# Layer two's K projection at one Strassen level for seven pairs of token tiles instead of four, and the layer norm of its last tiles applied by ScalarE

## The chip, the cores and the metric

The kernel runs on one core of a Trainium2 chip. The core has five engines, and each works through a queue of its own in program order: TensorE (PE, with its weight loads shown apart as PEld), VectorE (DVE), ScalarE (ACT), GpSimd (POOL) and SyncE (SP), which here issues all transfers to the 16 DMA engines. Work is passed between the engines by semaphores. PSUM is the memory into which TensorE writes, eight banks of 128x512 values in f32; SBUF is the working memory ("arena" in the profile).

The metric is the device time of one launch in microseconds (us), lower being better. The time before is 1434.43 us, the median of three runs.

## The reference, cut to what matters

Two blocks, linear attention (A) and a gated bilinear unit (B), each behind a layer norm and with a residual, are run twice with the same weights. There are 2048 tokens of 1024 features.

```python
def _A_ref(x, wqkv, wo):                      # x is normalised
    q, k, v = split(x @ wqkv)                 # 32 heads of 32
    phi = lambda t: jnp.where(t > 0, t + 1, jnp.exp(t)) + 1e-6
    pq, pk = phi(q), phi(k)
    kv = jnp.einsum("bhsd,bhse->bhde", pk, v)
    z = jnp.einsum("bhsd->bhd", pk)
    num = jnp.einsum("bhqd,bhde->bhqe", pq, kv)
    den = jnp.einsum("bhqd,bhd->bhq", pq, z)[..., None] + 1e-6
    return merge_heads(num / den) @ wo

def _layernorm(x, axis=-1, eps=1e-5):
    m = jnp.mean(x, axis=axis, keepdims=True)
    v = jnp.var(x, axis=axis, keepdims=True)
    return (x - m) / jnp.sqrt(v + eps)

x = A_x
x = x + _A_ref(_layernorm(x), A_wqkv, A_wo)
x = x + _B_ref(_layernorm(x), B_w_gate, B_w_up, B_w_down)
x = x + _A_ref(_layernorm(x), A_wqkv, A_wo)
x = x + _B_ref(_layernorm(x), B_w_gate, B_w_up, B_w_down)
```

## The kernel before

**How the program is put together.** Python code calls `P.add(engine, ...)` for every piece of work, with the memory that it reads and writes. The order of these calls is the order of each engine's queue; the waits between engines follow from the memory ranges. Nothing reorders a queue later. So where an instruction stands in the code decides what stands behind it.

**The stage that the change touches** is the projection of K and Q in layer two, `kq_pairs(0)` (L1025) under `layer_A` (L963). The 2048 tokens are 16 tiles of 128, taken in the order 4, 5, 6, 7, 0 to 3, 12 to 15, 8 to 11, two at a time: pairs 0 to 7. A pair is done in one of two ways.

- `plain` (L1101): four steps, one for each tile and each half of 512 output columns. A step is eight matmuls of 128x512 (`proj2`, L969), an exponential on ScalarE (`ex`, L1062) and, for the K side, one pair of VectorE instructions of 128x1024 for each tile (`fin2_`, L1077: the minimum, L657, and the sum that gives phi, L1085).
- `strassen` (L1151): one Strassen level, seven steps of four matmuls (L1167), in the order of products 1, 5, 6, 2, 7, 3, 4. Banks A, B, C and D of PSUM hold the four blocks. Step 0 multiplies into A, and ScalarE copies A to B (L1179 for K, L1177 for Q). Step 1 multiplies into C with a difference of weight blocks, T(0), and ScalarE copies C to SBUF (`p5`, L1183). Step 2 adds to B, and VectorE's `join` (L1171) writes D = B + `p5`. Step 3 adds to A, which is then complete. Step 4 adds to B and `join` writes C = B + `p5`. Step 5 adds to D, step 6 to B. Each complete block gets an exponential on ScalarE and, one block at a time, the minimum (L657 for K, L655 for Q's first block; Q's other three need none) and phi (L1096) on VectorE (`fin1_`, L1090).

TensorE may go on from step 2 to step 4 only when the first `join` has read B, and from step 4 to step 6 only when the second `join` has. A `fin` isn't put on VectorE's queue at once: it waits in a list (`pend`), and is queued after the next K or Q step, or ahead of any step numbered 0 (`flush`).

Before the change, K pairs 0 to 3 are plain (`KP0 = 4`), K pairs 4 to 7 and Q pairs 0 to 6 go by Strassen. The order is written out in `KQ_SEQ[False]` (L199). A token is one call: `K21` is step 1 of K pair 2, `Q` likewise; `S20` to `S23` are VectorE's four sums of token blocks for pairs 2 and 3 (`s_sums`, L1127); `X` loads a normalised tile back from DRAM; `V`, `W` and `O` load the next weights; `L` is one step of layer norm.

**A step of layer norm** (`flow_step`, L641, of class `LN`) works on four tiles at once, each a stage apart: it starts the transfer that transposes one tile, applies the norm to the next (`ln_b2`, L505), works out the variance of the one after that (`ln_b1`, L490) and the sum of a fourth (`ln_a`, L468). In this stage the sum (L473) and the sum of squares (L493) are ScalarE's, the few 128x1 values between them GpSimd's (L475, L495, L497), and the application is VectorE's (L507). Elsewhere a tile whose statistics come from VectorE is applied by ScalarE (L511). `lnp.on_act` chooses between the two, read when `ln_b1` is queued. When the stage begins, tile 8 (counted in the order above) is being applied, tile 9 has its variance and tile 10 its sum; tiles 10 to 15 are finished by the first eight `L` of the stage, and the others find nothing to do.

**The weight differences T(0) to T(3)** were worked out once in layer one and stored to DRAM (`pt_scratch`). Layer two loads them at the end of the block before it (`dticks1`, `load_t`), Q's four and then K's four, K's in two transfers of 1024 KB: T(0) with T(1), T(2) with T(3). SyncE issues them behind 3.5 MB of other weights and Q's four differences, and ahead of eight stores of x.

**The other place** is the output stage of layer one (L1488 to L1507), where `nxt.on_act` is true and the last tiles' sums already come from ScalarE (`nxt.stat_act = first and i > 11`). There too `ln_b2` took VectorE's L507 whenever the statistics were ScalarE's.

Of the kernel before, what the change touches and what calls it, by code (L numbers as in the profile page):

```python
# [180 lines left out]
def build_kernel(nc, A_x, A_wqkv, A_wo, B_w_gate, B_w_up, B_w_down, out):  # L181
# [14 lines left out]
    KSTR = True  # L196
    NEB = 3
    KQ_SEQ = {True: "L S30 Q20 S31 T L K30 S32 K31 L K32 Q21 S33 L Q22 K33 T S40 Q23 Q30 K40 K41 S41 L K42 Q31 Q32 Q33 L S42 K43 L Q34 K50 L Q35 Q36 S50 S43 K51 L Q40 L S51 S52 K52 Q41 Q42 Q43 L K53 Q44 Q45 L K60 Q46 K61 S60 Q50 S53 K62 Q51 S61 Q52 S62 Q53 Q54 K63 Q55 Q56 K70 Q60 K71 Q61 S63 Q62 L K72 Q63 Q64 Q65 K73 Q66 V",
              False: "K00 S00 S01 K01 S02 S03 L K02 K03 K10 L X K11 Q00 K12 Q01 X L Q02 K13 Q03 Q04 K20 X S20 Q05 S21 K21 S22 L Q06 S23 Q10 K22 X Q11 Q12 K23 Q13 L K30 X Q14 S40 Q15 S41 K31 S42 Q16 S43 Q20 X L K32 Q21 Q22 K33 Q23 X K40 Q24 L K41 Q25 K42 Q26 X K43 Q30 K44 K45 L Q31 K46 X Q32 Q33 K50 Q34 S60 K51 Q35 S61 L X S62 K52 S63 Q36 K53 Q40 K54 Q41 X K55 Q42 L K56 Q43 K60 Q44 K61 X Q45 K62 Q46 K63 L Q50 K64 X Q51 K65 Q52 K66 Q53 K70 L X Q54 K71 Q55 K72 Q56 K73 X Q60 K74 L Q61 K75 Q62 K76 Q63 X Q64 L Q65 Q66 V W O"}  # L199
    L1P0 = 3  # L200
    L1QS = 3
    QLAG = 0.409
# [3 lines left out]
    SPOS = 0.867  # L206
    SSTEP = 0.063
    CUP = 9
    KP0 = 4

    L2SETS = {(False, 0): "15", (False, 1): "15", (True, 0): "1532", (True, 1): "1532"}
    ORDERS = {
# [10 lines left out]
    def take(n, align=64):  # L223
        nonlocal off
        off = (off + align - 1) // align * align
        o = off
        off += n
        return o
# [10 lines left out]
    O_MV = [take(64) for _ in range(8)]  # L239
# [51 lines left out]
    P = _Prog(V_PT + 64)  # L291
# [42 lines left out]
    with ExitStack() as es:  # L334
# [10 lines left out]
        def vb(o, n):  # L345
            return ab[:, o // 2: o // 2 + n]
# [4 lines left out]
        def vf(o, n):  # L351
            return af[:, o // 4: o // 4 + n]
# [31 lines left out]
        mv = [vf(o, 5) for o in O_MV]  # L384
# [37 lines left out]
        def R(o, n):  # L422
            return [(o, o + n)]

        def r_x(i, lo=0, hi=D):
            return [(O_X + (i * D + lo) * 2, O_X + (i * D + hi) * 2)]
# [16 lines left out]
        def mset(ap, v, rng):  # L443
# [5 lines left out]
              rd=R(O_A[0], 1024), pwr=[B_KVT[1]])  # L449
# [8 lines left out]
        for h in range(4):  # L458
# [4 lines left out]
              rd=R(O_IDENT, 256), wr=R(O_IDENT, 256))  # L463
# [26 lines left out]
        def ln_b1(i, j, on_act, act=False, oj=0):  # L490
            junk = vb(oj, D)
            if act:
                P.add("act", lambda e: e.activation(junk, x_res[:, i, :], AF.Square, bias=mv[j][:, 0:1], accum_out=mv[j][:, 1:2]),  # L493
                      rd=r_x(i) + R(O_MV[j], 4), wr=R(oj, D * 2) + R(O_MV[j] + 4, 4))
                P.add("pool", lambda e: e.tensor_scalar(out=mv[j][:, 2:3], in0=mv[j][:, 1:2], scalar1=1.0 / D, scalar2=EPS_LN, op0=ALU.mult, op1=ALU.add),  # L495
                      rd=R(O_MV[j] + 4, 4), wr=R(O_MV[j] + 8, 4))
                P.add("pool", lambda e: e.tensor_tensor(out=mv[j][:, 3:4], in0=mv[j][:, 2:3], in1=mhalf, op=ALU.pow),  # L497
                      rd=R(O_MV[j] + 8, 4) + R(O_MHALF, 4), wr=R(O_MV[j] + 12, 4))
                return
            if on_act:  # L500
                P.add("dve", lambda e: e.tensor_scalar(out=mv[j][:, 4:5], in0=mv[j][:, 0:1], scalar1=mv[j][:, 3:4], scalar2=-1.0,
                                                        op0=ALU.mult, op1=ALU.mult),
                      rd=R(O_MV[j], 4) + R(O_MV[j] + 12, 4), wr=R(O_MV[j] + 16, 4))

        def ln_b2(i, j, dst, r_dst, on_act, act=False):  # L505
            if act:
                P.add("dve", lambda e: e.tensor_scalar(out=dst, in0=x_res[:, i, :], scalar1=mv[j][:, 0:1], scalar2=mv[j][:, 3:4],  # L507
                                                        op0=ALU.add, op1=ALU.mult),
                      rd=r_x(i) + R(O_MV[j], 4) + R(O_MV[j] + 12, 4), wr=r_dst)
            elif on_act:  # L510
                P.add("act", lambda e: e.activation(dst, x_res[:, i, :], AF.Identity, bias=mv[j][:, 4:5], scale=mv[j][:, 3:4]),  # L511
                      rd=r_x(i) + R(O_MV[j] + 12, 8), wr=r_dst)
            else:
                P.add("dve", lambda e: e.tensor_scalar(out=dst, in0=x_res[:, i, :], scalar1=mv[j][:, 0:1], scalar2=mv[j][:, 3:4],
                                                        op0=ALU.subtract, op1=ALU.mult),
                      rd=r_x(i) + R(O_MV[j], 4) + R(O_MV[j] + 12, 4), wr=r_dst)
# [446 lines left out]
        def layer_A(lnp, nxt, first, pro):  # L963
# [61 lines left out]
            def kq_pairs(p0):  # L1025
# [234 lines left out]
                else:  # L1260
                    for p in range(NP_):
                        st_ = plain("k", p) if p < KP0 else strassen("k", p)
                        for n, f in enumerate(st_):
# [4 lines left out]
                    for p in range(0, NP_, 2):  # L1268
                        for n in range(4):
                            at((p - SPOS if p >= KP0 else p + 1 - SPOS) + SSTEP * n, "S%d%d" % (p, n), lambda p=p, n=n: s_do(p, n, 2))  # L1270
                    for n in range(14):
# [56 lines left out]
                lnp.start(2)  # L1328
            else:
                lnp.use_dma = True  # L1330
            lnp.stat_act = not first

            def pt_ops(n):
                w = "kq".index(n)
# [1010 lines left out]
```

## Time and profile before

| what | value |
|---|---|
| time, median of three runs | 1434.43 us (1433.94 to 1434.46) |
| the profiled execution's own time | 1432.3 us |
| its span, first to last instruction | 1430.6 us |
| PE busy | 1420.2 us, 99% |
| DVE busy | 1167.1 us, 82% |
| ACT busy | 733.5 us, 51% |
| POOL busy | 314.6 us, 22% |
| the K and Q stage of layer two | from 730.24 us to 824.23 us of the span |

Starts in a timeline are microseconds from the first instruction. A line of a timeline gives the start, the duration, the engine, the line of the code, the operation, the memory written and read, the number of merged instructions, and, in brackets, how long the engine had been idle before and what ended that. Instructions of one engine overlap a little at their ends, so the cost of one in a full queue is the distance from its start to the next one's start. "idle" of an engine that has nothing to do is no loss; only what holds up the last engine costs time.

### The profile page before, as it was taken

To read this page: it belongs to the slowest core of one execution; us is meant where nothing else is said; L and a number is where in the kernel's file an instruction comes from. 1 tells how busy PE (TensorE), PEld (TensorE's weight loads), DVE (VectorE), ACT (ScalarE), POOL (GpSimd) and SP (SyncE) were. 2 spreads that over 40 slices of the span, in tenths; PEclk is the share of its full clock that TensorE was granted. 3 is DMA by queue.
4 is the path that set the end of the run, shared out by engine and by line. 5 is a ranking of instruction groups with operands and counts; after the bars stand their busy time and mean duration, and the time that the engine had idled before them with its cause. 6 is when DMAs were issued, how large, how long until landed. Compare 5 with 4: busy or idle time off the path is not lost.

```text
span 1430.6 us, 22386 instructions
## 1 busy us (share of the span) xinstructions
PE 1420.2 (99%) x8332; PEld 809.8 (57%) x8388; DVE 1167.1 (82%) x2012; ACT 733.5 (51%) x1538; POOL 314.6 (22%) x321
## 2 busy tenths in 40 slices
PE   9999999999999999999999999999999999999999
PEld 4444444555544555554764444456666477666658
DVE  7878887888879799878778878779877877777886
ACT  4752367767621255552256523667776116777521
POOL 5644632000013000003334346301000400000160
PEclk9999999999999999999999999999999999999999
DMA  6316867987878899985998067589976699788668
GB/s 235 106 28 182 182 137 195 289 294 251 290 253 286 296 324 303 293 260 171 262 355 220 27 178 162 137 229 273 287 253 200 224 299 317 255 261 265 207 187 259
DMA packets 393997, 330.15 MB, mean 231 GB/s; under 512 B 178337, under 2 KB 342049, under 8 KB 393377
## 3 DMA queue, kind: packets, MB, share of 16 engines
q1 hardware_dynamic: 393888, 328.72, 77.0%
q8 instruction: 66, 1.08, 0.3%
q14 instruction: 43, 0.34, 0.1%
HBM read 238.49 MB, written 66.58 MB: 213 GB/s over the span
## 4 chain that ended last, share of the span: by engine, by line
PE 95%; DVE 2%; ACT 1%; issue 1%; POOL 1%; DMA 0%; SPq 0%; ACTq 0%
PE ps L1593 27%; PE ps L1668 18%; PE ps L2109 14%; PE ps L2017 8%; PE ps L1499 8%; PE ps L1401 8%; PE ps L1167 6%; PE ps L971 4%; PE ps L981 2%; PE ps L1413 1%; ACT arena L493 0%; DVE arena L841 0%; DMA arena<-in_A_x_dram 0%; PE ps L1441 0%; ACT arena L473 0%
## 5 line engine op out<-in xcount | busy, mean ns | idle before, releaser
L841 DVE TENSOR_TENSOR arena<-arena 128x512 f16<-128x512 f16 (+9 forms) x780 | 480.5, 644 | 76.4 <-ACT arena L1712 45.1
L1593 PE MATMUL ps<-arena 128*128 128x512 f16 x1808 | 446.8, 379 | 0.6 <-ACT ps L1623 0.6
L1668 PE MATMUL ps<-arena 128*128 128x256 f16 x2324 | 312.1, 273 | 0.7 <-ACT arena L1712 0.6
L844 DVE SCALAR_TENSOR_TENSOR arena<-ps,arena 128x512 f16<-128x512 f32 (+2 forms) x392 | 259.9, 685 | 38.8 <-PE ps L1593 16.3
L1668 PEld LDWEIGHTS ps<-arena 128*128 128x128 f16 (+1 forms) x2324 | 226.4, 98 | 104.0 <-DVE ps L1687 3.8
L1593 PEld LDWEIGHTS ps<-arena 128*128 128x128 f16 (+1 forms) x1808 | 176.5, 98 | 141.7 <-ACT ps L1623 1.1
L2062 POOL TENSOR_TENSOR arena<-arena 128x512 f32<-128x512 f32 x56 | 87.4, 1565 | 596.5 <-ACT arena L2060 591.5
L2109 PE MATMUL ps<-arena 128*128 128x512 f16 (+1 forms) x941 | 205.7, 379 | 0.6
L1598 ACT ACTIVATE arena<-ps 128x512 f16<-128x512 f32 x224 | 134.0, 598 | 91.8 <-PE ps L1593 89.8
L2109 PEld LDWEIGHTS ps<-arena 128*128 128x128 f16 x952 | 93.2, 98 | 111.5
L1684 ACT COPY ps<-ps 128x256 f32<-128x256 f32 x220 | 81.0, 368 | 79.8 <-PE ps L1668 73.4
L1687 DVE TENSOR_TENSOR ps<-ps,arena 128x256 f32<-128x256 f32 x220 | 92.3, 428 | 34.5 <-PE ps L1668 18.3
L2017 PE MATMUL ps<-arena 128*128 128x256 f16 (+1 forms) x1078 | 119.0, 273 | 0.1
L1401 PE MATMUL ps<-arena 128*128 128x512 bf16 x499 | 114.1, 379 | 0.7
L2017 PEld LDWEIGHTS ps<-arena 128*128 128x128 f16 x1078 | 104.9, 98 | 13.9 <-DVE ps L2024 0.4
L1499 PE MATMUL ps<-arena 128*128 128x512 bf16 x500 | 110.7, 379 | 0.6
L2060 ACT ACTIVATE arena<-ps 128x512 f32<-128x512 f32 x48 | 28.7, 597 | 132.6 <-PE ps L2109 132.6
L1167 PE MATMUL ps<-arena 128*128 128x512 bf16 (+1 forms) x412 | 94.7, 379 | 0.8 <-DVE ps L1171 0.3
L1307 POOL TENSOR_TENSOR arena<-arena 128x1024 f16<-128x1024 f32 x32 | 80.0, 2501 | 69.5 <-DVE arena L1305 62.3
L1623 ACT COPY ps<-ps 128x512 f32<-128x512 f32 x112 | 64.2, 573 | 50.2 <-PE ps L1668 44.8
L1006 POOL TENSOR_TENSOR arena<-arena 128x512 f32<-128x512 f32 x60 | 73.6, 1245 | 69.4 <-DVE arena L1096 33.6
L1499 PEld LDWEIGHTS ps<-arena 128*128 128x128 f16 x512 | 50.1, 98 | 59.8
(80 smaller groups left out, 1262.0 us busy)
## 6 DMA issues: line engine op xcount, KB each, us to landing
arena<-w_scratch SPq DMA_DIRECT2D x84, 512.0 KB, 5.2
arena<-sp_scratch SPq DMA_DIRECT2D x56, 512.0 KB, 5.8
arena<-t_scratch SPq DMA_DIRECT2D x27, 896.0 KB, 5.8
arena<-in_B_w_down_dram SPq DMA_DIRECT2D x18, 896.0 KB, 6.2
w_scratch<-arena SPq DMA_DIRECT2D x28, 512.0 KB, 6.0
sp_scratch<-arena SPq DMA_DIRECT2D x28, 512.0 KB, 4.4
arena<-in_B_w_gate_dram SPq DMA_DIRECT2D x42, 256.0 KB, 5.1
arena<-in_B_w_up_dram SPq DMA_DIRECT2D x42, 256.0 KB, 3.4
```

The source lines that it names most:

```text
L841: P.add("dve", lambda e: e.tensor_tensor(out=out, in0=a, in1=b, op=op), rd=rd, wr=wr, prd=prd)
L844: P.add("dve", lambda e: e.scalar_tensor_tensor(out=out, in0=a, scalar=sc, in1=b, op0=ALU.mult, op1=op1), rd=rd, wr=wr, prd=prd)
L1167: P.add("pe", lambda e: [e.matmul(psb(bank), x[:, k, :], w[:, k, :], start=(start and k == 0), stop=(k == 3), skip_group_check=True) for k ...
L1401: return [e.matmul(psb(bank), xr[:, t, j * 128:(j + 1) * 128], pk[:, h, t, :], start=(t == 0), stop=(t == NST - 1)) for t in range(NST)]
L1499: return [e.matmul(psb(bank), xnT[:, g, i * 128:(i + 1) * 128], wp[:, g, dh * 512:(dh + 1) * 512], start=(dh == 0 and g == 0), stop=(g == ...
L1593: P.add("pe", lambda e: [e.matmul(psb(bank), w[:, k, :], x[:, k, :], start=(start and k == 0), stop=(k == 3), skip_group_check=True) for k ...
L1598: P.add("act", lambda e: e.activation(t, psb(bank), AF.Copy, scale=SG), prd=[bank], wr=r)
L1668: P.add("pe", lambda e: [e.matmul(psb(bank)[:, 256 * half:256 * half + 256], w[:, k, :], xx[:, k, :], start=(start and k == 0), stop=(k == ...
L1687: P.add("dve", lambda e: e.tensor_tensor(out=psb(dst[c])[:, 256:512], in0=lo, in1=c5, op=ALU.add), prd=[bk], rd=rc5, pwr=[dst[c]])
L2017: P.add("pe", lambda e: [e.matmul(psb(bank)[:, 256 * half:256 * half + 256], a[:, k, :], w[:, k, :], start=(start and k == 0), stop=(k == ...
L2062: P.add("pool", (lambda k2, x: lambda e: e.tensor_tensor(out=rtmp[k2], in0=rtmp[k], in1=x, op=ALU.add))(k2, x), rd=rx + rr(k), wr=rr(k2))
L2109: return [e.matmul(psb(bank), hv[:, 7 * hf + k, t * 128:(t + 1) * 128], w[:, k, :], start=(start and hf == 0 and k == 0), stop=(hf == 1 an ...
```

## The change

`KP0` becomes 1, so K pairs 1, 2 and 3 go by Strassen too. The written order changes with it. `lnp.on_act` becomes true for the layer norm of layer two's attention, and `ln_b2` obeys it also for tiles whose statistics ScalarE made; `ln_b1` then adds a GpSimd product of two 128x1 values, the bias for ScalarE's instruction.

```diff
     KQ_SEQ = {True: ...
-              False: "K00 S00 S01 K01 S02 S03 L K02 K03 K10 L X K11 Q00 K12 Q01 X L Q02 K13 Q03 Q04 K20 X S20 Q05 S21 K21 S22 L Q06 S23 Q10 K22 X Q11 Q12 K23 Q13 L K30 X Q14 S40 Q15 S41 K31 S42 Q16 S43 Q20 X L K32 Q21 Q22 K33 Q23 X K40 Q24 L K41 Q25 K42 Q26 X K43 Q30 K44 K45 L Q31 K46 X Q32 Q33 K50 Q34 S60 K51 Q35 S61 L X S62 K52 S63 Q36 K53 Q40 K54 Q41 X K55 Q42 L K56 Q43 K60 Q44 K61 X Q45 K62 Q46 K63 L Q50 K64 X Q51 K65 Q52 K66 Q53 K70 L X Q54 K71 Q55 K72 Q56 K73 X Q60 K74 L Q61 K75 Q62 K76 Q63 X Q64 L Q65 Q66 V W O"}
+              False: "K00 S00 S01 K01 S02 S03 L K02 K03 K10 L X K11 K12 X L K13 Q00 K14 S20 K15 S21 Q01 S22 K16 X S23 Q02 Q03 K20 L Q04 K21 Q05 X K22 Q06 K23 X Q10 K24 L K25 S40 Q11 S41 K26 S42 Q12 S43 Q13 K30 X Q14 K31 L Q15 K32 Q16 K33 X Q20 K34 L K35 Q21 K36 X Q22 Q23 K40 Q24 L K41 Q25 X K42 Q26 K43 L Q30 K44 K45 Q31 S60 K46 S61 Q32 X S62 Q33 S63 K50 Q34 L K51 Q35 X K52 Q36 K53 Q40 L K54 X K55 Q41 K56 Q42 Q43 K60 Q44 L K61 Q45 X K62 Q46 K63 L Q50 K64 X K65 Q51 K66 Q52 Q53 K70 L Q54 K71 Q55 K72 X Q56 K73 Q60 X K74 K75 Q61 K76 Q62 Q63 Q64 Q65 Q66 V W O"}
...
-    KP0 = 4
+    KP0 = 1
...
         def ln_b1(i, j, on_act, act=False, oj=0):
...
+                if on_act:
+                    P.add("pool", lambda e: e.tensor_tensor(out=mv[j][:, 4:5], in0=mv[j][:, 0:1], in1=mv[j][:, 3:4], op=ALU.mult),
+                          rd=R(O_MV[j], 4) + R(O_MV[j] + 12, 4), wr=R(O_MV[j] + 16, 4))
                 return
...
         def ln_b2(i, j, dst, r_dst, on_act, act=False):
-            if act:
+            if act and not on_act:
                 P.add("dve", lambda e: e.tensor_scalar(out=dst, in0=x_res[:, i, :], scalar1=mv[j][:, 0:1], scalar2=mv[j][:, 3:4],
                                                         op0=ALU.add, op1=ALU.mult),
...
             elif on_act:
                 P.add("act", lambda e: e.activation(dst, x_res[:, i, :], AF.Identity, bias=mv[j][:, 4:5], scale=mv[j][:, 3:4]),
...
-            lnp.stat_act = not first
+            lnp.stat_act = lnp.on_act = not first
```

## The prediction

> **What bounds the kernel now.** I read the page first, then the chain of waits around layer two's K and Q stage, then the timelines of ScalarE, GpSimd and VectorE in it, then the landing times of the transfers.
>
> ```profile
> PE 1420.2 (99%) x8332; PEld 809.8 (57%) x8388; DVE 1167.1 (82%) x2012; ACT 733.5 (51%) x1538; POOL 314.6 (22%) x321
> ...
> 730.24 10.31 PE ps L971 x47
> ...
> 741.41 1.73 PE ps L971 x8
> ...
> 820.89 3.50 PE ps L1167 x15
> 824.39 6.91 PE ps L1401 x32
> ```
>
> TensorE sets the time, and in this stage it never pauses: the chain stays on it from the first K matmul at 730.24 to the G matmuls that follow. Eight matmuls of 128x512 take 1.73 us, 0.216 each. Everything else in the stage is hidden, so the question is what the change uncovers.
>
> **What it removes.** A plain pair has 32 matmuls, a Strassen pair 28. K pairs 1 to 3 save 12 x 0.216 = **2.6 us**. This is all there is to win, since no other engine ends the stage; and 0.2% of the time, about what a measurement of this kernel can tell from no change, is 2.9 us.
>
> **The weight differences.** Step 1 of a K Strassen pair multiplies with T(0). Before the change the first such step is K41, 208 matmuls into the stage (about 775). Now it is K11, behind K00 to K03 and K10: 36 matmuls, 730.24 + 36 x 0.216 = 738.0. Two rows on each transfer give its issue and the time from there to its landing:
>
> ```profile
> L441 SPq DMA_DIRECT2D arena<-pt_scratch x1: 432/432/432, 731.1 to 731.1; - x1
> DMA to landing us min/median/max: 12.0/12.0/12.0
> ...
> L441 SPq DMA_DIRECT2D arena<-pt_scratch x1: 432/432/432, 731.5 to 731.5; - x1
> DMA to landing us min/median/max: 14.0/14.0/14.0
> ...
> DMA  9999999999999999999999999999359989999898
> ```
>
> The first is K's T(0) and T(1): there at 743.1. The second is T(2) and T(3): 745.5. The DMA engines are nine tenths busy or more over that time (the last row, 715 to 765), and the change issues nothing earlier. So K11 stands **5.1 us** at the head of TensorE's queue with everything behind it. K16, the first user of T(3), comes after 745.5 anyway. Bounds: nothing (if the landing is read too late) to 5.1.
>
> **ScalarE's queue.** One `L` and what follows it, and the instruction that the change moves to ScalarE, in layer two's output stage:
>
> ```profile
> 739.35 1.14 ACT L493 ACTIVATE arena<-arena 128x1024 bf16<-128x1024 bf16 x1
> 740.39 0.19 ACT L493 ACTIVATION_READ_ACCUMULATOR arena<-arena 128x1 f32 x1
> 740.61 1.06 ACT L473 ACTIVATE arena<-arena 128x1024 bf16<-128x1024 bf16 x1
> 741.67 0.58 ACT L1069 ACTIVATE arena<-ps 128x512 bf16<-128x512 f32 x1
> ...
> 905.34 1.24 ACT L511 ACTIVATE arena<-arena 128x1024 f16<-128x1024 bf16 x1 [2.98 <-DVE arena L501]
> 906.49 0.56 ACT L1507 CAST arena<-ps 128x512 bf16<-128x512 f32 x1
> ...
> 806.07 0.60 ACT L1069 ACTIVATE arena<-ps 128x512 bf16<-128x512 f32 x1 [0.94 <-DVE ps L1171]
> 806.56 0.58 ACT L1183 COPY arena<-ps 128x512 f32<-128x512 f32 x1
> ```
>
> From start to start: L493 takes 1.26 us, L473 1.06, L511 1.15, an exponential or a copy 0.5. An `L` on ScalarE grows from 2.3 to **3.5 us**, for tiles 10 to 15 (tile 9's variance is queued before `on_act` is set), and each new Strassen pair adds two copies: 6 x 1.15 + 6 x 0.5 = 9.9 us, nearly all before step K34. ScalarE's load there now:
>
> ```profile
> 730.00:740.00 10.00, 9.95 (x48) 4.53 (x48) 8.06 (x13) 7.43 (x14) 3.74 (x9) 1.00 1.06 394
> 740.00:750.00 10.00, 9.95 (x47) 4.56 (x47) 5.32 (x8) 7.52 (x15) 7.67 (x11) 1.00 1.26 386
> 750.00:760.00 10.00, 9.95 (x47) 4.45 (x46) 8.24 (x13) 7.04 (x13) 5.48 (x7) 1.00 0.91 246
> 760.00:770.00 10.00, 9.95 (x47) 4.55 (x47) 9.53 (x14) 8.23 (x16) 4.17 (x6) 1.00 0.85 198
> ```
>
> The columns are the stretch's length, then PE, PEld, DVE, ACT and POOL busy. ACT has 30.2 of 40 us. With 9.9 more in 2.6 us less it is full, so it falls behind, and steps that wait for it come late.
>
> **VectorE's queue**, from these starts:
>
> ```profile
> 808.53 0.28 DVE L657 TENSOR_SCALAR arena<-arena 128x512 bf16<-128x512 bf16 x1
> 808.85 0.69 DVE L1096 SCALAR_TENSOR_TENSOR arena<-ps,arena 128x512 bf16<-128x512 f32 x1
> 809.46 0.28 DVE L657 TENSOR_SCALAR arena<-arena 128x512 bf16<-128x512 bf16 x1
> ...
> 751.79 1.41 DVE L841 TENSOR_TENSOR arena<-arena 128x1024 f16<-128x1024 f16 x2
> L1171 DVE TENSOR_TENSOR ps<-ps,arena 128x512 f32<-128x512 f32 x22 | 15.3, 693 | 1.7 <-PE ps L1167 1.4
> L1085 DVE SCALAR_TENSOR_TENSOR arena<-ps,arena 128x1024 bf16<-128x1024 f32 x8 | 9.8, 1225 | 0.3
> L657 DVE TENSOR_SCALAR arena<-arena 128x1024 bf16<-128x1024 bf16 x8 | 3.5, 440 | 8.5 <-ACT arena L1069 8.5
> L507 DVE TENSOR_SCALAR arena<-arena 128x1024 f16<-128x1024 bf16 x7 | 4.7, 667 | 0.0
> ```
>
> The timeline's rows give starts; the other four are the groups of the window 730 to 824.5, with count, busy time and mean ns. A block's `fin` takes 0.93 (0.32 + 0.61), a `join`, whose duration equals the phi instruction's, 0.61 as well, a sum S 0.7. Six tiles' fins (6 x 1.67) become twelve blocks' (12 x 0.93), 1.1 more, and six joins add 3.7; six applications take 6 x 0.67 = 4.0 away. So VectorE's work stays within 1 us of what it was, and that is no bound. What matters is that a `join` stands behind `fin`s that wait for late exponentials.
>
> **The walk** puts the new order through the four queues with these durations.
> - Pair 1: T lets K11 run from 743.1, `p5` is copied by 744.5. The `L` ahead of K13 fills ScalarE to 747.95. K13's exponential is done at 748.45, its `fin` at 749.4, and only then can K14's `join` run, to 750.05. K16, due at 749.15, waits 0.95.
> - S20 to S23 and two fins (4 x 0.7 + 2 x 0.93) and then Q02's `join` take VectorE to 755.3. Q04, due at 753.5, waits 1.75.
> - Pair 2: K20's copy waits for K16's `fin` in bank B, with an `L` of 3.5 us behind the copy; K24 waits 0.7 for its `join`. The next `L` stands ahead of K25's exponential and Q11's `p5`; behind these on VectorE are K25's `fin`, S41, S42 and Q12's `join`, done at 772.2. Q14, due at 768.2, waits 4.0.
> - Pair 3, in the same way: K36 waits 1.4, Q24 0.3. Then no `L` finds work, and the order is nearly that of before; I count nothing, up to 1 us at the end, where Q62 to Q66 follow each other.
>
> Sum behind the T wait: **9.1 us**. From below it is bounded by nothing (the `L`s fall into the pause for T), from above by ScalarE's whole addition and the S sums crowded into pair 1, about 13. I take the walk, because each of its waits is a queue order that the code fixes, with durations of the same instructions.
>
> ```profile
> 739.63 2.50 POOL L1006 TENSOR_TENSOR arena<-arena 128x512 f32<-128x512 f32 x2 [1.62 <-DVE arena L1085]
> ...
> 742.20 0.19 POOL L495 TENSOR_SCALAR arena<-arena 128x1 f32<-128x1 f32 x1
> 742.47 0.66 POOL L497 TENSOR_TENSOR arena<-arena 128x1 f32<-128x1 f32 x1
> ```
>
> What else moves is covered. GpSimd's extra product, another two-operand instruction of that shape, adds some 0.6: tile 11's is ready at 743.7, before ScalarE comes free for it at 744.5 (without the pause for T it would hold ScalarE up by 1.2). The `xn_scratch` store and the transpose behind it on SP now wait for ScalarE, but S40 needs them some 15 us later, and the `X` loads queued behind are needed in the G stage.
>
> **Layer one's output stage** changes too: tiles 11 and 12 are applied by ScalarE.
>
> ```profile
> 231.66 0.58 ACT L1493 CAST ps<-arena 128x512 f32<-128x512 bf16 x1
> ...
> 238.40 0.59 ACT L1507 CAST arena<-ps 128x512 bf16<-128x512 f32 x1 [0.67 <-PE ps L1499]
> ...
> 243.46 1.90 PE L1593 MATMUL ps<-arena 128*128 128x512 f16 x8 [0.58 <-ACT ps L1623]
> ```
>
> ScalarE is full from 231.66 to 237.7 and has 0.67 us to spare ahead of 238.40; from there the chain runs over it to 243.46, where TensorE already waits. Two times 1.15 less 0.67 is **1.6 us** (0 to 2.3).
>
> **Sum**: -2.6 + 5.1 + 9.1 + 1.6 = +13.2. On the profiled execution's own 1432.3 us (span 1430.6) that is 1445.5; it lies 2.1 under the median of 1434.43, on whose scale it is 1447.6. I forecast **1446.5**, own range 1442 to 1450.
>
> **Rivals.**
> - *Only the transfer counts* (20%): in the 5.1 us pause ScalarE works off its queue and never falls behind again. -2.6 + 5.1 + 1.6 = +4.1, about 1437.5. For it: ACT is below 83% of every stretch now. Against: three later `L`s stand right ahead of a copy or an exponential.
> - *The clock* (10%): pauses of 5.1 and 4.0 us are longer than any here. A cold TensorE is seen at the start:
>
> ```profile
> 1.37 4.45 PE L448 MATMUL ps<-arena 128*128 128x512 f16 x10 [1.37 <-POOL arena L444]
> PEclk9999999999999999999999999999999999999999
> ```
>
>   Ten matmuls took 4.45 us where 2.16 is the later pace. One or two such restarts would add 2.3 to 4.6, partly hidden by the late ScalarE: about 1450. The granted clock is 9 in every slice, so no run here shows a restart. The Trainium skill ("TensorE: Matmul & The Clock Gate", Part 1) says that after an idle window of about 3.4 us the clock halves until a window of work has passed; by that both pauses could trigger it, about 1.7 us each as an estimate from that page.
> - *Not slower* (13%): K's T(0) is in SBUF by 738.0, so that K11 doesn't wait, and no `L` delays a `join`. Then only -2.6 is left: about 1431. It decides at one point, whether the first transfer lands before K10 ends. Against it: it would have to land 5.1 us sooner than in the trace, with the DMA engines full.
> - Faster by more than 0.2% (2%) would need more than the 12 matmuls.
>
> My forecast has 55%. The range, **1436.5 to 1451**, leaves out the third rival and the tails. Faster by over 0.2%: 0.02; within: 0.14 (the third rival and the lowest part of the first); slower: 0.84.
>
> **What would show it.** In the profile after: TensorE idle about 5 us ahead of L1167 at 738, released by a DMA of `pt_scratch`; further pauses of TensorE released by L1171 (VectorE) between 749 and 785; ACT near full from 743 to 780; the G matmuls starting at about 824.2 + 13. If TensorE runs through at 738, the step on the transfer is wrong; if it pauses only there, the walk is.

## The result, and the profile after

The kernel after the change takes 1456.3 us (median of four runs, 1455.69 to 1460.42) where the kernel before takes 1434.18 (four runs). It is **slower by 22 to 24 us**: the two medians differ by 22.1, while the measured ratio, 1.0168 with a 95% interval of 1.0155 to 1.0181, is 24.1 us on the 1432.3 of the kernel before in the runs below. A kernel that differs from the one after only by idle matmuls (a4, below) lost 24.0. The forecast of 1446.5 had the sign and missed the size: 1456.3 lies outside its range, which ended at 1451.

The profiled execution is the longest of the four (1460.42; the other three lie within 0.7 of each other), so lengths of stages are compared, not whole spans. Lines of the code from L499 on have moved down by three: L1167 is now L1170, L1171 (`join`) L1174, L841 (the sums S) L844, L657 L660, L1006 L1009.

Two rows of the page of the kernel after, engines and granted clock by slice:

```profile
PE 1428.3 (98%) x8376; PEld 808.8 (55%) x8376; DVE 1173.2 (80%) x2022; ACT 745.0 (51%) x1552; POOL 315.5 (22%) x329
...
PEclk9999999999999999999989999999999999999999
```

TensorE no longer runs through: a 98 in place of 99%, and one slice of the clock shows 8 where all had 9. TensorE's own timeline says where. A row begins after a pause if it has a bracket: how long TensorE was idle, and who ended that.

```profile
238.33 1.90 PE L1502 MATMUL ps<-arena 128*128 128x512 bf16 x8 [1.03 <-ACT ps L1496]
244.92 1.04 PE L1596 MATMUL ps<-arena 128*128 128x512 f16 x4 [1.23 <-ACT arena L1601]
...
258.16 0.83 PE L1671 MATMUL ps<-arena 128*128 128x256 f16 x6 [0.85 <-DVE ps L1690]
283.31 0.83 PE L1671 MATMUL ps<-arena 128*128 128x256 f16 x6 [1.43 <-DVE ps L1690]
...
735.54 7.07 PE L974 MATMUL ps<-arena 128*128 128x512 bf16 x32
742.45 1.03 PE L1170 MATMUL ps<-arena 128*128 128x512 bf16 x4
748.07 12.31 PE L1170 MATMUL ps<-arena 128*128 128x512 f16 x44 [4.59 <-DMA arena<-pt_scratch]
762.61 13.95 PE L1170 MATMUL ps<-arena 128*128 128x512 f16 x56 [2.24 <-DVE ps L1174]
781.42 10.15 PE L1170 MATMUL ps<-arena 128*128 128x512 f16 x40 [4.86 <-DVE ps L1174]
792.32 3.63 PE L1170 MATMUL ps<-arena 128*128 128x512 f16 x16 [0.75 <-DVE ps L1174]
796.22 12.26 PE L1170 MATMUL ps<-arena 128*128 128x512 f16 x56 [0.28 <-DVE ps L1174]
809.48 3.63 PE L1170 MATMUL ps<-arena 128*128 128x512 f16 x16 [1.00 <-DVE ps L1174]
815.05 34.96 PE L1170 MATMUL ps<-arena 128*128 128x512 f16 x160 [1.94 <-DVE ps L1174]
849.87 2.32 PE L1404 MATMUL ps<-arena 128*128 128x512 bf16 x10
```

The first four rows are layer one's output stage and the stage behind it, the others the K and Q stage. From its first K matmul to the first G matmul it takes 849.87 - 735.54 = **114.3 us**; before it took 94.0. Counting the matmuls from row to row gives the step behind each pause: K11, Q04, Q14, K36, Q24, Q34, Q36. The transfer stands at the head as forecast (4.6, forecast 5.1), and the six pauses that follow, 0.28 to 4.86, are all ended by a `join`.

A listed pause is smaller than its loss. A matmul's row is 0.379 long while the next one starts 0.216 later, and the idle time counts from the modelled end: 0.16 more is lost at each pause. The seven pauses sum to 15.7, with that to 16.8. The 12 matmuls saved put the stage at 91.4, so 22.9 is lost, and some 6 of that is in no pause. The windows of the kernel after show it (columns as in the prediction; the last three are the granted clock, the busy share of the DMA engines and GB/s):

```profile
740.00:750.00 10.00, 5.41 (x22) 2.11 (x20) 3.23 (x4) 7.19 (x13) 5.70 (x12) 0.83 1.01 413
750.00:760.00 10.00, 10.00 (x40) 4.16 (x38) 6.07 (x11) 7.62 (x13) 2.47 (x6) 0.83 1.16 295
760.00:770.00 10.00, 7.76 (x29) 3.05 (x28) 6.73 (x11) 6.55 (x12) 4.84 (x7) 0.83 0.94 258
770.00:780.00 10.00, 6.56 (x31) 2.75 (x29) 6.92 (x12) 6.92 (x12) 3.62 (x6) 1.00 0.30 79
```

Two things are to be seen. The granted clock falls to 0.83 in stretches behind pauses: from 750 to 760 TensorE is busy all the time and has 40 matmuls, where it had 47 before. And over these 40 us **no engine is full**: ACT has 28.3 of them, less than the 30.2 of 40 before the change, and DVE 23.0. In windows of 5 us the two take turns:

```profile
750.00:755.00 5.00, 5.00 (x16) 1.90 (x15) 1.14 (x3) 4.97 (x8) 1.19 (x4) 0.65 1.33 369
755.00:760.00 5.00, 5.00 (x25) 2.25 (x23) 4.93 (x9) 2.65 (x6) 1.29 (x2) 1.00 0.99 222
765.00:770.00 5.00, 5.00 (x20) 2.08 (x19) 1.80 (x4) 4.97 (x10) 2.00 (x5) 0.79 0.81 226
```

ScalarE is full in the first and the third (4.97), VectorE in the second (4.93), and in between each waits for the other: VectorE 2.15 us for an exponential (L1072, to 754.52), ScalarE 1.14 us for a `join` (L1174, to 756.18).

### The profile page after: what moved, and what is told of

The parts are those of the page before. It is cut to its first block, busy times and chain, and to the rows that moved or that the text cites. A ratio compares the mean times of both kernels' runs of the same rounds, so it can differ in the third digit from the quotient of the medians.

```text
span 1458.7 us, 22455 instructions
## 1 busy us (share of the span) xinstructions
PE 1428.3 (98%) x8376; PEld 808.8 (55%) x8376; DVE 1173.2 (80%) x2022; ACT 745.0 (51%) x1552; POOL 315.5 (22%) x329
## 4 chain that ended last, share of the span: by engine, by line
PE 85%; DVE 6%; DMA 3%; ACT 3%; issue 1%; SPq 1%; POOL 1%; DVEq 0%
PE ps L1596 25%; PE ps L1671 17%; PE ps L2112 14%; PE ps L1404 8%; PE ps L2020 7%; PE ps L1502 6%; PE ps L1170 4%; DVE arena L844 2%; PE ps L984 2%; PE ps L974 2%; DMA arena<-in_B_w_down_dram 1%; DVE arena L1099 1%; SPq L441 1%; DMA arena<-pt_scratch 1%; ACT arena L493 1%
## 5 line engine op out<-in xcount | busy, mean ns | idle before, releaser
L844 DVE TENSOR_TENSOR arena<-arena 128x512 f16<-128x512 f16 (+9 forms) x780 | 484.1, 649 | 80.6 <-ACT arena L1715 45.1
L1170 PE MATMUL ps<-arena 128*128 128x512 bf16 (+1 forms) x504 | 118.6, 393 | 16.0 <-DVE ps L1174 11.4
L2020 PEld LDWEIGHTS ps<-arena 128*128 128x128 f16 x1078 | 104.6, 98 | 16.6 <-DMA arena<-in_B_w_down_dram 1.0
L1170 PEld LDWEIGHTS ps<-arena 128*128 128x128 f16 x504 | 49.8, 101 | 82.6 <-DVE ps L1174 16.4
L1009 POOL TENSOR_TENSOR arena<-arena 128x512 f32<-128x512 f32 x60 | 74.4, 1255 | 75.4 <-DVE arena L1099 50.2
```

The costliest lines, as they stand in the source:

```text
L844: P.add("dve", lambda e: e.tensor_tensor(out=out, in0=a, in1=b, op=op), rd=rd, wr=wr, prd=prd)
L1170: P.add("pe", lambda e: [e.matmul(psb(bank), x[:, k, :], w[:, k, :], start=(start and k == 0), stop=(k == 3), skip_group_check=True) for k ...
L2020: P.add("pe", lambda e: [e.matmul(psb(bank)[:, 256 * half:256 * half + 256], a[:, k, :], w[:, k, :], start=(start and k == 0), stop=(k == ...
```

## The experiments

Eighteen kernels were run, in six groups. "Loss" is the median less that of the kernel before on the same chip (1432.3 to 1432.9; for the kernel after, the difference of the medians and what its ratio gives). "Stage" is from the first K to the first G matmul in the one profiled execution, "pauses" those listed there of 0.3 or more, with their steps where it matters.

| run | loss, us | ratio, 95% | stage | pauses in the stage |
|---|---|---|---|---|
| before | 0 | | 94.0 | none |
| after | 22.1, 24.1 | 1.0155-1.0181 | 114.3 | 4.59 DMA, 2.24, 4.86, 0.75, 1.00, 1.94 |
| a1 order alone | 17.3 | 1.0104-1.0138 | 110.9 | 4.98 DMA, 2.09, 3.62, 0.99, 1.94 |
| a2 norm alone | 5.9 | 1.0024-1.0050 | 96.3 | 1.84 ACT |
| a3 norm in layer one alone | 4.2 | 1.0018-1.0040 | 94.0 | none |
| a4 pauses filled | 24.0 | 1.0151-1.0182 | 113.6 | below |
| b1 K's T first | 22.3 | 1.0139-1.0173 | 114.2 | 2.63 DMA, 1.87, 2.78, 4.85, 0.64, 0.99, 1.95 |
| c1 sums moved | 19.4 | 1.0119-1.0149 | 109.9 | 4.72 DMA, 0.79, 5.50, 0.35, 0.56 |
| c4 norm cut short | 16.6 | 1.0101-1.0131 | 106.5 | 4.86 DMA, 1.85, 2.17, 0.38, 0.99, 1.94 |
| d2 K pairs 2, 3 only | 2.5 | 1.0007-1.0026 | 96.2 | 0.64, 0.70 ACT, 0.46 ACT |
| e1 GpSimd's additions out | 18.5 | 1.0108-1.0139 | 110.1 | 0.35 DMA (K01), 5.66 DMA, 0.89, 0.73, 3.79 |
| e2 three repairs | 11.1 | 1.0065-1.0093 | 105.5 | 3.15, 1.39, 4.37, 0.35, 0.56 |
| e3 K pair 3 only | 4.9 | 1.0023-1.0048 | 99.5 | 3.12, 0.47 ACT |
| e4 a3, load ahead | 7.2 | 1.0040-1.0065 | 94.2 | none |
| f1 all eased | 8.0 | 1.0041-1.0068 | 97.0 | 2.62 DMA, 0.65 |
| f2 layer two alone | 21.1 | 1.0133-1.0160 | 114.2 | 4.75 DMA, 2.78, 5.22, 0.99, 1.94 |
| f3 e2, filled | 11.3 | 1.0063-1.0091 | 104.1 | 0.37, 1.39, 0.38, 0.41, 0.36, 0.56 |
| f4 a3, stores ahead | 3.7 | 1.0015-1.0036 | 94.0 | none |
| g1 e3, filled | 4.7 | 1.0026-1.0054 | 98.0 | 1.59 |
| g2 e3, later sums | 2.2 | 1.0008-1.0025 | 96.7 | 0.61, 0.30, 0.46 ACT |

### The change taken apart: a1, a2, a3, f2

a1 is the kernel after with the norm as before (the three edits of `ln_b1`, `ln_b2` and `on_act` undone). a2 has the norm edits alone, with `KP0 = 4` and the old order. a3 is a2 without

```diff
-            lnp.stat_act = lnp.on_act = not first
+            lnp.stat_act = not first
```

so that only layer one's two tiles are applied by ScalarE; f2 is the kernel after with those two alone left on VectorE.

> The new order and KP0 = 1, with the layer norm as before (VectorE applies). Theory (the transfer of T, the queues of ScalarE and VectorE, and the cold clock behind long pauses add up): K11 still waits 4.6 to 5.1 us, an L costs ScalarE 2.3 us and not 3.5, so the waits for joins fall from about 11 us to 5 or so, the cold clock to half, and layer one loses nothing: about 1445 (1441 to 1449). Rival (the layer norm's move to ScalarE is harmless, the order alone does it): 1455 to 1456, as after.

> The order of before and KP0 = 4, with the layer norm's edits of the change. Theory: in the old order ScalarE has room for six more instructions of 1.15 us (30.2 of 40 us busy) and few steps depend on what stands behind an L, so layer two loses 0 to 2 us; layer one loses what its own experiment shows: 1436 to 1441 in all. Rival (harmless everywhere): 1434. Rival (the norm is the main loss): over 1445.

> Before, with only layer one's two tiles (11 and 12 of the output stage) applied by ScalarE. The prediction's term: +1.6 us, 1435.8. The trace of after, where TensorE pauses at L1496, L1601 and twice for VectorE in the next stage: +3 to +5, 1437 to 1439.

> The kernel after the change with layer one's two tiles normalised on VectorE as before it. Theory (layer one's loss and the stage's lie behind each other on TensorE and add): 4.2 less than the kernel after the change, about 1452. Rival (the later start of the stage lets its queues and transfers catch up, so that part of layer one's loss is absorbed there): 1453.5 to 1456.

The new order loses 17.3 with no norm on ScalarE at all, the norm 5.9 without the new order; 17.3 + 5.9 = 23.2 lies between the two figures of the whole loss. a1's 1449.6 is 0.6 above its theory's range: its waits for joins sum to 8.6 and not to 5. Of a2's 5.9, 4.2 are layer one's. In f2 the pauses of 1.03 and 1.23 are gone from layer one, and the stage is as long as that of the kernel after (114.2). Its 1454.0 lies in the rival's range; its time is lower by 3.0 in the ratios (1.0147 for 1.0168), where the theory had 4.2. The intervals leave open whether the stage absorbs some of it. For the stage itself, the longer `L` on ScalarE, which the prediction's walk set first, is worth 3.4 us (114.3 against 110.9), and the order, with its joins and the transfer, the rest.

### The pauses filled: a4, f3, g1

a4 puts 20, 8 and 16 matmuls that nobody reads ahead of K11, Q04 and Q14, so that TensorE doesn't fall idle for long:

```diff
-... K10 L X K11 K12 ... K20 L Q04 K21 ... K30 X Q14 K31 ...
+... K10 L X F20 K11 K12 ... K20 L F8 Q04 K21 ... K30 X F16 Q14 K31 ...
```

> After, with matmuls into a bank that is overwritten next put into three pauses: 20 ahead of K11, 8 ahead of Q04, 16 ahead of Q14, so that TensorE is not idle there for over 3 us. The waits stay. If the cold clock costs its about 7 us of the stage on top of the waits: about 1449, granted clock 1.0 through the stage. If a slow TensorE only fills time in which VectorE and ScalarE are late anyway: 1454 to 1456 with the clock at 1.0 and longer waits for joins.

TensorE's timeline of a4; L1288 are the added matmuls:

```profile
742.29 4.48 PE L1288 MATMUL ps<-arena 128*128 128x512 bf16 x19
747.40 6.20 PE L1170 MATMUL ps<-arena 128*128 128x512 f16 x28 [0.63 <-DMA arena<-pt_scratch]
754.70 3.63 PE L1170 MATMUL ps<-arena 128*128 128x512 f16 x16 [1.09 <-DVE ps L1174]
758.38 1.67 PE L1288 MATMUL ps<-arena 128*128 128x512 bf16 x7
761.11 6.22 PE L1170 MATMUL ps<-arena 128*128 128x512 f16 x28 [1.05 <-DVE ps L1174]
768.05 6.35 PE L1170 MATMUL ps<-arena 128*128 128x512 f16 x27 [0.73 <-DVE ps L1174]
774.24 3.62 PE L1288 MATMUL ps<-arena 128*128 128x512 bf16 x16
779.91 3.63 PE L1170 MATMUL ps<-arena 128*128 128x512 f16 x16 [2.05 <-DVE ps L1174]
783.92 5.35 PE L1170 MATMUL ps<-arena 128*128 128x512 f16 x23 [0.38 <-DVE ps L1174]
790.81 3.63 PE L1170 MATMUL ps<-arena 128*128 128x512 f16 x16 [1.54 <-DVE ps L1174]
794.71 12.26 PE L1170 MATMUL ps<-arena 128*128 128x512 f16 x55 [0.28 <-DVE ps L1174]
807.97 3.63 PE L1170 MATMUL ps<-arena 128*128 128x512 f16 x16 [0.99 <-DVE ps L1174]
813.53 31.69 PE L1170 MATMUL ps<-arena 128*128 128x512 f16 x143 [1.94 <-DVE ps L1174]
```

The mean clock rises from 0.995 to 0.999, and the time is the same: ratio 1.0166 for 1.0168. The 7 us that the first theory put on the clock aren't there; TensorE would have spent them, or nearly all of them, waiting. f3 fills two pauses of e2 (14 matmuls ahead of K14, 20 ahead of Q14), g1 the one pause of 3.1 in e3 (13 ahead of K31).

> The run e2 (three repairs, 1443.6) with 14 idle matmuls ahead of K14 and 20 ahead of Q14, so that TensorE does not fall idle there. Theory (where VectorE is no longer late behind a pause, the slowed clock does cost time: in e2 the stage is 105.5 long, 91.5 for its matmuls at full clock and 10.1 for its pauses): the clock stays full, stage 102 to 103, about 1441. Rival (as in a4, other engines would be late by as much, so that the clock costs nothing): 1443 to 1444.

> The run e3 (K pair 3 at one level too, 1437.4) with 13 idle matmuls ahead of K31, which fill its pause of 3.1 us. Theory (a restart of the clock behind a pause that stands alone costs time: there 64 matmuls took 1.7 more than at full clock): the clock stays full, and the time falls by 1 to 2, to about 1435.5 to 1436.5. Rival (VectorE is late behind that pause anyway, so that the full clock only makes later waits): no change, 1437 or more.

The times are those of the rivals: 1.0077 for e2's 1.0079, and 1.0040 for e3's 1.0036, with the clock at 1.0. But these intervals reach some 2 us to either side, and in the one profiled execution of each the filled stage is the shorter by 0.7 (a4), 1.4 (f3) and 1.5 us (g1). So the 7 us are excluded; whether a restart behind a pause costs the 1 to 2 us that the theories of f3 and g1 gave it stays open.

a4 also shows the waits bare, since no slow matmul covers them. A filled pause is its idle time and 0.216 for each added matmul:

| step | K11 | K16 | Q04 | K24 | Q14 | Q16 | K36 | Q24 | Q34 | Q36 |
|---|---|---|---|---|---|---|---|---|---|---|
| walk | 5.1 | 0.95 | 1.75 | 0.7 | 4.0 | 0 | 1.4 | 0.3 | 0 | 0 |
| a4 | 4.9 | 1.1 | 2.8 | 0.7 | 5.5 | 0.4 | 1.5 | 0.3 | 1.0 | 1.9 |

The sum is 4.9 + 15.2 in place of 5.1 + 9.1. With 0.16 for each of the ten and less 2.6 it gives 19.1; the stage of a4 is 113.6 - 94.0 = 19.6 longer. The sum closes to half a microsecond.

### The transfer, the sums and ScalarE: b1, c1, c4

b1 loads K's weight differences ahead of Q's. c1 moves S20 to S23 right behind K10 and spreads S61 to S63 over the steps up to K53:

```diff
-... K03 K10 L X ... K14 S20 K15 S21 Q01 S22 K16 X S23 Q02 ... K46 S61 Q32 X S62 Q33 S63 K50 ...
+... K03 K10 S20 S21 S22 S23 L X ... K14 K15 Q01 K16 X Q02 ... K46 Q32 X Q33 S61 K50 ... Q35 S62 ... K53 S63 ...
```

c4 lets the three ScalarE instructions of an `L` (L473, L493, L514) work on 16 columns in place of 1024; layer two's statistics and normalised tiles are then not computed.

> After, with K's T(0) and T(1) loaded first of the five loads of weight differences, T(2) and T(3) fourth. K11's wait for the transfer falls from 4.6 to 5.1 us to about 1.5. If the transfer's wait adds to the others: about 1452.5. If ScalarE's and VectorE's queues, which get no pause to catch up in, take its place: the waits for joins grow by as much, 1455 to 1456.

> After, with S20 to S23 queued right behind K10 (where VectorE idles while TensorE waits for T) and S61, S62, S63 spread over Q33 to K53. If crowded sums on VectorE make Q04, Q34 and Q36 late: these three waits (2.2 to 2.8, 1.0 and 1.9 us) go, 1451 to 1453. If those joins are late for ScalarE's sake, nothing changes: 1456.

> After, with the three ScalarE instructions of an L in layer two cut from 1024 to 16 columns (so the statistics and the normalised tiles of that layer are left out). K11's wait for T stays at about 5 us. If ScalarE's time in the L's is what makes the joins late at K16, K24, Q14 and K36: these waits fall under 1 us each, the stage falls from 114 to about 100 us, 1441 to 1445. If VectorE's own work is the bound: 1450 or more.

b1: K11 no longer waits, K14 waits 2.63 for the second transfer, and the time doesn't move beyond the intervals (1.0156). New waits for joins take the place, 1.87 at K16 and 2.78 at Q04 where 2.24 stood. c1 gains 4.4 us in the stage: Q04's pause goes and one of 0.79 stands at K24, Q14's grows from 4.86 to 5.50, K36's goes, Q34's 1.00 goes and Q36's 1.94 falls to 0.35, with a new 0.56 at K56. That these two stood unchanged at 0.99 and 1.94 in a1, b1, c4 and f2, whatever was done to ScalarE or to the transfer, while c1, which moves only VectorE's sums, nearly removes them, says that they are VectorE's own. c4 gains 7.8 in the stage, Q14's pause falling from 4.86 to 2.17. Its 1449.4 lies between its two theories: Q04's 1.85 and Q14's 2.17 did not fall under 1. So ScalarE counts, but with all three of its norm instructions, two of which it had before, and it is not the whole.

### VectorE beside GpSimd: e1

Each phi of a K block is followed by GpSimd's addition into `z` (L1009). e1 leaves those out but for the first tile's.

> The kernel after the change with GpSimd's additions of K in layer two's K and Q stage left out, apart from those of the first tile (that part of K is not computed). Theory (VectorE is held while GpSimd works on SBUF): the S sums take 0.7 us again in place of 1.6, the shortest 128x512 normalisation 0.28, the pauses ahead of Q04, Q14, Q34 and Q36 shrink, and the stage from the first K matmul to the first G matmul falls from 114.3 to 107 to 110; about 1449 to 1452. Rival (the S sums are long for a reason of their own, or VectorE would wait for late exponentials anyway): stage 113 to 114, about 1455 to 1456.

VectorE's groups in the stretch 735 to 835, count, busy time and mean ns; first of the kernel after:

```profile
L844 DVE TENSOR_TENSOR arena<-arena 128x1024 f16<-128x1024 f16 x16 | 14.8, 953 | 0.1
L660 DVE TENSOR_SCALAR arena<-arena 128x512 bf16<-128x512 bf16 x24 | 9.2, 382 | 8.4 <-ACT arena L1072 8.4
L658 DVE TENSOR_SCALAR arena<-arena 128x512 bf16<-128x512 bf16 x5 | 3.3, 666 | 0.0
```

and the same groups of e1:

```profile
L844 DVE TENSOR_TENSOR arena<-arena 128x1024 f16<-128x1024 f16 x16 | 10.5, 683 | 0.1
L660 DVE TENSOR_SCALAR arena<-arena 128x512 bf16<-128x512 bf16 x24 | 6.9, 289 | 8.7 <-ACT arena L1074 8.4
L658 DVE TENSOR_SCALAR arena<-arena 128x512 bf16<-128x512 bf16 x6 | 1.7, 284 | 0.0
```

Sixteen sums took 0.95 each in place of 0.68, 24 minima 0.38 in place of 0.29, five others 0.67 in place of 0.28: 4.3 + 2.2 + 1.9 = 8.4 us of VectorE's time. Before the change the same reckoning over its own rows

```profile
L841 DVE TENSOR_TENSOR arena<-arena 128x1024 f16<-128x1024 f16 x12 | 8.9, 745 | 0.0
L657 DVE TENSOR_SCALAR arena<-arena 128x512 bf16<-128x512 bf16 x16 | 4.9, 308 | 2.8 <-ACT arena L1069 2.7
L655 DVE TENSOR_SCALAR arena<-arena 128x512 bf16<-128x512 bf16 x7 | 4.7, 670 | 0.0
```

gives 0.7 + 0.3 + 2.7 = 3.7. The theory held: without the additions the stage is 4.2 shorter (110.1, at the end of the forecast 107 to 110), although K11 waits 1.1 longer in that execution. Q04's pause falls from 2.24 to 0.89, with one of 0.73 at K24, and those at Q34 and Q36 are all but gone (0.15 and none). Of Q14's 4.86, 3.8 stays. The two engines side by side in the kernel after, VectorE's timeline and then GpSimd's:

```profile
759.10 0.69 DVE L1099 SCALAR_TENSOR_TENSOR arena<-ps,arena 128x512 bf16<-128x512 f32 x1
759.71 2.24 DVE L844 TENSOR_TENSOR arena<-arena 128x1024 f16<-128x1024 f16 x2
```

```profile
755.63 1.16 POOL L1009 TENSOR_TENSOR arena<-arena 128x512 f32<-128x512 f32 x1 [1.31 <-DVE arena L1099]
759.87 1.53 POOL L1009 TENSOR_TENSOR arena<-arena 128x512 f32<-128x512 f32 x1 [3.09 <-DVE arena L1099]
```

Two sums take 2.24 where two alone take 1.41, and GpSimd's addition 1.53 in place of 1.16. The addition is released by the phi ahead of it (L1099), so it begins just as VectorE's next instruction does. The change puts other neighbours there: the phis of half a tile are followed by sums and minima, where plain pairs had the phi of a whole tile next.

### Repairs, and how far they go: e2, f1, d2, e3, g2

e2 is seven pairs at one level with the norm on VectorE (a1), the loads of b1 and the order of c1. f1 is the kernel after with c4's, e1's, b1's and c1's edits together; it leaves out what c4 and e1 leave out.

> Seven pairs at one Strassen level with the three repairs at once: the normalisations on VectorE as before, K's weight differences loaded first, the sums S20 to S23 right behind K10 and S61 to S63 spread. Theory (transfer, ScalarE's share, crowded sums and the rest of VectorE's queue are separate waits): pauses of about 2.6 for the transfer and 2 to 4 ahead of Q14, none over 1 us ahead of Q04, Q34 and Q36; stage 98 to 103, about 1438 to 1443, so that it is still slower than the kernel before. Rival (the repairs win back all that is late): stage 92 to 93, about 1431 to 1432. Second rival (each wait that goes makes the next one longer, as the earlier load did): stage 106 or more, 1446 or more.

> The kernel after the change with everything eased at once in layer two's K and Q stage: ScalarE's three normalisation instructions on 16 columns in place of 1024 (statistics and normalised tiles are not computed), GpSimd's additions of K left out apart from the first tile's, K's weight differences loaded first, the sums S20 to S23 behind K10 and S61 to S63 spread. Layer one as after the change. Theory (these four hold all of the stage's loss): the stage takes 92 to 95, one pause of up to 2.6 for the transfer and small ones; about 1434.5 to 1438, of which some 4 are layer one's. Rival (VectorE's plain load of joins and half-tile evictions is a cause of its own): stage 97 or more, about 1440 or more, with pauses that VectorE ends.

e2 came out between its theory and the second rival: stage 105.5, Q14 still waits 4.4, loss 11. f1's stage of 97.0 and its 1440.9 are the figures of its rival, but its pauses are those of the theory (2.62 for the transfer, 0.65 for the join ahead of Q14). Of the 2 us that remain of 97.0 - 91.4, about 1.7 are slow clock behind the transfer's pause: the 84 matmuls there take 19.95 us, where 84 x 0.216 is 18.1, and the clock reads 0.80 and 0.86 in 745 to 755. No run fills that pause, so this cost is read from the trace alone. So the four causes together hold 17.3 of the stage's 20.3, and beside the 0.65 VectorE's plain load of joins and half-tile phis shows as no cause of its own. Of f1's 8.0, 3.0 are the stage's; most of the rest is layer one's.

Could fewer pairs pay? d2 is the kernel before with K pairs 2 and 3 at one level too, e3 with pair 3 alone, g2 is e3 with its sums later:

```diff
-... K23 S40 Q13 L K30 S41 X Q14 K31 S42 Q15 K32 S43 Q16 ...
+... K23 Q13 L K30 X Q14 K31 S40 Q15 S41 K32 S42 Q16 K33 S43 ...
```

> Before, norm applied by VectorE, with KP0 = 2: K pairs 2 and 3 by Strassen, in an order that keeps every L behind a step whose copies are done, S20 to S23 spread over pair 1. T is in SBUF long before K21. If the waits of after come from the places of L, S and T: no wait over 0.5 us, the stage 92.3 us against 94.0, 1430.5 to 1433 (no measurable difference). If two Strassen pairs there are too much for ScalarE and VectorE in any order: waits for joins of 2 us or more, 1434 to 1440.

> The kernel before with K pair 3 alone at one Strassen level as well, and its sums S40 to S43 ahead of it; normalisations on VectorE. Theory (VectorE has no room for a further pair's joins in this stretch): the 4 matmuls saved, 0.86 us, are given back in pauses of TensorE that VectorE or ScalarE end; stage 94 to 95.5, about 1432.5 to 1434.5. Rival (one pair fits, and the loss of the whole change comes only from three at once): stage 93.1 with no pause, about 0.9 us less than the kernel before.

> The run e3 with the sums S40 to S43 behind K31 and later, where the transposed tile that they read has landed. Theory (e3's loss is that sum at the head of VectorE's queue, not the further pair): its pause of 3.1 goes, the stage falls from 99.5 to 93 to 94.5, and the time lies within 1 us of the kernel before, on either side. Rival (the further pair's joins leave VectorE late in any order): pauses of 2 us or more remain, 1435 or more.

None is faster than the kernel before. d2's 1435.2 lies in its second range, but without the waits of 2 us that went with it: five pauses of 0.18 to 0.70 eat the 1.7 of its 8 matmuls and more. e3 has one row of VectorE's timeline that explains most of its 4.9:

```profile
764.50 0.69 DVE L841 TENSOR_TENSOR arena<-arena 128x1024 f16<-128x1024 f16 x1 [4.36 <-DMA arena<-arena]
```

The sum S40 stood at the head of VectorE's queue before the transposed tile that it reads had landed, and everything behind it waited. g2 puts it behind K31: the pause goes, and the loss falls to 2.2. It does not fall to nothing: small pauses, mostly ended by a `join`, eat the 0.86 of the four matmuls and more. The theory was right on the cause and too hopeful on the rest.

### Layer one: e4, f4

a3's loss of 4.2 is more than its pauses of 1.03 and 1.23. SyncE's timeline, before and then in a3 (whose span starts 1.6 later here):

```profile
228.98 7.68 SPq L592 DMA_TRANSPOSE arena<-arena  x3
236.71 4.09 SPq L441 DMA_DIRECT2D x_scratch<-arena  x7
240.84 0.64 SPq L441 DMA_DIRECT2D arena<-in_B_w_down_dram  x1
```

```profile
230.62 11.53 SPq L595 DMA_TRANSPOSE arena<-arena  x3
242.19 4.10 SPq L441 DMA_DIRECT2D x_scratch<-arena  x7
246.33 0.65 SPq L441 DMA_DIRECT2D arena<-in_B_w_down_dram  x1
```

The transposes wait for the tiles that ScalarE now applies, and hold the stores of x and a load behind them on the queue 3.9 longer. e4 issues the load ahead of the stores; f4 writes the stores ahead of the tiles' transposes in the code.

> Layer one's two normalisations on ScalarE alone, as in the run a3, with the first load of w_down issued on SP ahead of the stores that wait for ScalarE. Theory (of a3's loss of 4.2 us, 2.3 are the two pauses behind ScalarE and the rest is VectorE waiting for w_down, whose load stood on SP behind transposes that waited for ScalarE): the pauses of 1.03 and 1.23 stay, those of 0.49 and 1.73 that VectorE ends go, and the loss is about 2.3. Rival (the later pauses come from ScalarE's added work or from VectorE's own queue): the loss stays at about 4.2.

> Layer one's two normalisations on ScalarE alone, as in a3, with the stores of x to DRAM issued on SP ahead of the three transposes that wait for ScalarE (the load of w_down stays behind them). Theory (a3's loss beyond its two ScalarE pauses, 1.03 and 1.23, is VectorE's additions waiting for those stores): the loss falls from 4.2 to between 2.3 and 3.5, and the later pauses that VectorE ends shrink. Rival (VectorE is late because its own normalisation waits for GpSimd, or because of the w_down load): the loss stays at 4.2 or more.

e4's theory fell: the loss grew to 7.2. VectorE's additions overwrite x, so they wait for the stores and not for the load, and with 1 MB ahead of them these land 6.2 us after their issue and not 2.8. VectorE's timeline of e4, where a3 has 1.63 and the kernel before 0.18 in the bracket:

```profile
249.56 3.68 DVE L844 TENSOR_TENSOR arena<-arena 128x256 f16<-128x256 bf16 x8 [6.07 <-DMA x_scratch<-arena]
```

f4 was a miss of another kind: the three transposes were queued earlier than the place where the stores were put, so every engine has a3's instructions in a3's order, and it is a repetition (3.7 after 4.2; its 8 runs reach from 1435.2 to 1437.6, a3's 7 from 1435.3 to 1438.8). In f4's profiled execution the later pauses that VectorE ends are 0.2, in a3's 0.5 and 1.7. VectorE starts equally late behind the stores in both (it waits 1.63 in a3, 1.65 in f4). What differs is its wait for the next load of w_down, in a3 and then in f4:

```profile
279.52 2.62 DVE L844 TENSOR_TENSOR arena<-arena 128x1024 f16<-128x1024 bf16 x4 [2.42 <-DMA arena<-in_B_w_down_dram]
275.59 2.62 DVE L844 TENSOR_TENSOR arena<-arena 128x1024 f16<-128x1024 bf16 x4 [0.46 <-DMA arena<-in_B_w_down_dram]
```

The kernel after has 2.12 there and the later pauses of 0.85 and 1.43. So the 2.3 of the two pauses behind ScalarE is in each of these profiles, and up to 2 more goes with how late that load lands, which varies from execution to execution. What the late stores add to it is not shown: no run has the stores ahead of the transposes.

## Why the prediction was right in kind and wrong in size

- **12 matmuls, -2.6**: holds by their number and the pace of 0.216; no run measures it apart.
- **The transfer, +5.1**: 4.6 to 5.7 in every run that left the loads in place, 4.9 in a4. Right, but not a price that can be taken off: in b1 half of it went and nothing was won.
- **The walk, +9.1: the step that failed.** Its mechanism is there: its waits at K16, K24, K36 and Q24 came to within 0.2 in a4. Part of that may be luck: K36's pause goes in a1 and c4, which ease ScalarE, as the walk has it, but also in c1 and e1, which leave ScalarE alone. Its size was 15.2. First, it priced a sum at 0.7 and a minimum at 0.32 "with these durations", as they run alone, and concluded of VectorE's work "that is no bound"; beside GpSimd's additions two sums take 2.24 and a minimum up to 1.25, which is what e1 took away (Q04 +1.0, and Q34 and Q36). The row of before had said it: L655's mean was 0.67, more than twice the 0.28 of that shape alone. Second, "Then no `L` finds work ... I count nothing" left out S60 to S63, crowded ahead of Q33 and Q36: 1.0 + 1.9, which c1 all but removed by spreading them. Third, Q14's 4.0 was 5.5; no single repair removed it (a1 3.6, e1 3.8, c4 2.2), and f1 left 0.65. Which cause holds which part of the 1.5 stays open.
- **ACT "near full from 743 to 780"**: wrong over the stretch. It had 25.4 of these 37 us, as much as before the change (25.3), and was full only in pieces of it (750 to 755, 765 to 770). The walk laid the lateness on ScalarE's longer `L`; undone, that gave 3.4 us back (a1). The joins are late because each stands behind fins, sums and minima that wait in turn: with the `L`s, the sums and the minima all eased, f1 has one pause for a join, 0.65. GpSimd's extra product took 0.2 and not 0.6, which changes nothing.
- **Ten starts**: each pause loses 0.16 beyond the listed idle time, 1.6 in all; not in the sum.
- **Layer one, +1.6** (0 to 2.3): 3.7 to 4.2. The two ScalarE pauses alone are 2.3, the upper end: the 0.67 to spare saved nothing. The rest is the later pauses, which go with the landing of w_down; the prediction looked at ScalarE alone there. SyncE's queue behind the transposes, which it named in layer two and not here, makes the stores late, and what that costs is not shown.
- **Rival "the clock"**: the restarts came, against "no run here shows a restart". Behind the 4.6 us pause the clock reads 0.66 and 0.65 in windows of 5 us, and behind e3's 3.12 us pause 64 matmuls take 15.56 us, 1.6 more than at 0.216 each; but in three filled runs the time doesn't fall beyond the intervals. The Trainium skill ("TensorE: Matmul & The Clock Gate", Part 1) says that idle time halves the clock until a window of work has passed; the rows fit that, and the 1.7 that the prediction worked out from it, but not the page's idle window of about 3.4 us, since f1's clock fell behind 2.62. The ten matmuls in 4.45 us that the prediction called cold stand where the granted clock reads 1.00, so the trace doesn't show that the clock slowed them.
- **Rival "only the transfer counts"**: fell; the pause did not give ScalarE the time to catch up.

13.2 + 6.1 (walk) + 1.6 (starts) + 2.6 (layer one) - 0.2 (transfer) = 23.3, against a measured 22.1 to 24.1.

## What to carry to other kernels

Price an instruction by what it takes next to its new neighbours, not alone: a group whose mean is twice its shortest row of the same shape may be held by another engine, and a reordering can make more of that. When a change adds hand-overs between in-order queues, walk the whole stage to its end, sums and stores included, because no engine need be full on the average for all of them to be late. A pause that is removed or a clock that is kept up is worth only what the next late engine leaves of it, so try the repairs together before adding up their prices.

## What the hardware showed that was not expected

- **GpSimd holds VectorE.** A VectorE sum of two tiles in SBUF took 0.68 alone and up to 1.64 beside a GpSimd addition (d2), a 128x512 bf16 minimum 0.28 alone and up to 1.25 (after); GpSimd's 1.16 became 1.53. VectorE's instructions that read PSUM kept their 0.69. The Trainium skill ("GPSIMD Engine Reference", Key points) says that the two engines share SBUF interfaces and contend for VectorE instructions with two SBUF inputs or in a two-port mode; the sums have two SBUF inputs, so the trace agrees there and adds the size; in which mode the minimum runs no run here shows.
- **The clock falls after short pauses and may cost little.** Behind 2.6 us of idle time (f1) the windows of 5 us show 0.80 and 0.86, behind 4.6 (after) 0.66 and 0.65. Filled with idle matmuls the clock stayed at 1.0 and the time did not change beyond its interval of some 2 us, three times (a4, f3, g1).
